# Four interleaved layers on one core: later loads allowed on ScalarE's queue, and a newly searched order

## The chip, the cores and the metric

One core of a Trainium2 chip runs the whole kernel. The metric is the device time of one execution in microseconds (us); smaller is better. The engines are TensorE (PE, with its weight loads PEld), VectorE (DVE), ScalarE (ACT), GpSimd (POOL) and SyncE (SP). SP and ACT begin transfers (DMAs) here.

## What is computed

Four layers in a row on x of 2048 rows and 512 columns: attention, linear attention, attention, linear attention, the second pair with the weights of the first. Both have 32 heads of 16 columns. Cut from the reference:

```python
def _A_ref(x, wqkv, wo):            # H = 32; Dh = 16; W = 256
    q, k, v = qkv[0], qkv[1], qkv[2]
    scores = jnp.einsum("bhqd,bhkd->bhqk", q, k) * (Dh ** -0.5)
    mask = (idx[:, None] - idx[None, :] >= 0) & (idx[:, None] - idx[None, :] < W)
    p = _softmax(jnp.where(mask[None, None], scores, -1e9), axis=-1)
    o = jnp.einsum("bhqk,bhkd->bhqd", p, v)
    return o @ wo                   # heads laid side by side
def _B_ref(x, wqkv, wo):
    phi = lambda t: jnp.where(t > 0, t + 1, jnp.exp(t)) + 1e-6
    pq, pk = phi(q), phi(k)
    kv = jnp.einsum("bhsd,bhse->bhde", pk, v)
    den = jnp.einsum("bhqd,bhd->bhq", pq, pk.sum(s))[..., None] + 1e-6
    return (jnp.einsum("bhqd,bhde->bhqe", pq, kv) / den) @ wo
x = x + _A_ref(_layernorm(x), A_wqkv, A_wo)
x = x + _B_ref(_layernorm(x), B_wqkv, B_wo)
x = x + _A_ref(_layernorm(x), A_wqkv, A_wo)
x = x + _B_ref(_layernorm(x), B_wqkv, B_wo)
```

## The kernel before

The rows are worked in 16 tiles of 128, four tiles to a block. Everything is laid down first as 2583 operations, each with the operations that it needs, the buffers that it holds and the engines that may run it. The string ORDER then says in which order they are emitted, on which engine (P, A, V, G, S for PE, ACT, DVE, POOL, SP; H is a mark for data that has landed) and in which buffer; "F" is a filler, a matmul on the identity whose result nobody reads (line 463). Each engine then runs its instructions strictly in that order, and waits where an instruction's inputs or buffers are not ready. A planner's costs in the code were used when the order was searched; they put nothing into the program.

**Attention.** Lines 806 to 857: q, k and v come from matmuls of 4 x 128 contraction rows (line 537) and are evacuated from PSUM by ACT or DVE (line 527 for q and v, lines 773, 786 and 788 for k, which is spread into two copies with the other head zeroed). 78 rounds per layer each compute scores (line 823, up to 512 columns in each of four banks), take the exponential in two ACT instructions (lines 834 and 837, up to 128x1024 each), and clear what the mask forbids, on POOL (line 857) or DVE (line 852). The weighted sum runs on PE (line 880); DVE normalises (lines 893, 894). Seven buffers pt hold the exponentials. v goes through a staging tile vst into vbd with four DMAs from SP (line 806), and o_sb is transposed into oT by a DMA from SP (line 557).

**Linear attention.** phi takes an exponential on ACT (line 948, 1024), a min/add on DVE or POOL (lines 951, 1027) and a max on DVE (954, 1030). The sums over rows (line 995) close with a chain: kvs (1002), zc and kvn (1042, 1051), the denominator (1078), its reciprocal on ACT (1083, 1084), its spreading (1106) and the product (1110), and last one projection for each tile. Parts of it run beside the next layer's attention.

**Layer norms.** Sums come from DVE (661, or with the residual at 736 to 738), squares from ACT (612, with a read of its accumulator) or DVE (614), the power from POOL (595, 596) or ACT (592, 593), the scaling from POOL (628, 675), DVE (628, 672) or ACT (626).

**Loads.** Four tiles of x and most of A's weights are begun before the order starts, on SP and ACT. The later loads, x tiles 8 to 15 (line 378) and wo of A, the weights and wo of B in halves of 256 KB (line 1133), are operations of their own, and all twelve begin on SP.

Of the kernel before, what the change touches and what calls it, by code (L numbers as in the profile page):

```python
# [214 lines left out]
24S 2G 5G 4G 15H 14H 53V0 0G 11G 58V1 17H 54A 68A1 6G 16H 63V2 3G 59G 55V20 18H 19H 1G 10F0 56P5 60V0 64G 61P1 57A 62V  # L215
9G 69V 2F2 74P0 75A 7V 1F2 70P1 65V0 72P6 71A 66P3 20H 92P7 73A 21H 67V 93P 120P42 94A 80P0 122A 95S 76P6 81V 88P1 121A
77V 89P 23H 22H 78P2 350V0 90A 123G 124P64 82P0 126A 79V 351G 91S 84P1 125A 340V1 133P24 83A 127G 96P6 85V 134A 106P0
10G 97V 104P1 135A 107V 137P26 341G 105V 139A 86P0 138A 146P46 87V 27S 116P1 147A 335V2 98P0 117P 148A 99V 336G 150P42
136V 25S 112P0 345V3 151A 149G 113P 152A 159P64 118A 337V31 140G 102P2 114V 161A 35S 128P1 346G 129P 103V 130P 131P 160A
342V1 163P42 153G 132V 26H 165A 115S 347V2 162G 3F0 188P06 164A 634V1 100P2 189A 166G 141P5 154P4 101V 155P 142P 36H  # L220
143P 190A 635G 144P 28H 352V0 193P02 145V 156P 119S 12G 157P 194A 108P6 158V 167P7 168P 191G 169P 195A 109V 170P 199P04
171V 348P6 200A 353P3 196G 349V 338P7 172S0 354V 343P6 201A 339V 204P02 638V0 379P7 29S 205A 380P 202G 344V 636V32 192G
206A 381V 2F5 210P04 361P6 639G 637S 642V1 362P 211A 208G 110P7 363V 212A 31S 203G 224P02 30H 198G 640V0 225A 383P5 213G
111V 384P 197V 382S 226A 643G 229P06 385V 214P4 215P 230A 646V0 216P 32H 358P5 644V3 231A 647G 217P 228V 235P02 641S
218V 359P 209G 236A 207G 355P7 360V 219P6 645S 237A 933V2 240P04 356P 241A 648V1 220P 239G 357V 221P 649S 232G 222P 233G
242A 246P02 227V 387P7 234G 386S 247A 223V 388P 238G 245V 389V 248A 395P04 13G 664P6 396A 665P 249V 934G 390S 250P7 667V
251P 397A 244G 400P02 666V 252P 243G 401A 941V0 253P 399G 391P6 392P 254V 402A 176S1 405P04 393V 364P7 406A 403G 365P
255P6 407A 366V 394S 410P02 256P 398V 257P 411A 404V 409G 258P 678P7 259V 412A 679P 416P04 680V 260S3 417A 657P3 414G
408V 415G 658P 276V 418A 650P2 264S2 660V 432P06 651P 413V 434A 419G 420V 51S 367P5 421V 368P 433A 659V 422P4 423P 369V
424P 653A 33S 436G 437P06 425P 438A 652V 427P5 428P 426V 429P 439A 430P 442P02 431V 376P4 443A 440G 377P 942G 34H 370P5  # L230
444A 378V 447P06 371P 441V 935V20 448A 682P4 372V 683P 449A 435V 453P02 684V 675P5 454A 676P 446V 451G 685S 452V 450V
455A 2F4 469P60 677V 445V 471A 457V 2F4 474P24 458V 456V 49S 937V1 475A 464P1 459P0 465P 476A 460P 466P 41S 461P 470A
467P 462P 479P24 463V 173P7 472G 480A 39S 468V 174P 481A 175V 484P02 654P6 945V2 936S 655P 485A 482G 373P7 473V 477G
656V 374P 938G 486A 681S 490P04 375V 690P6 483G 491A 691P 946G 487V 492A 177P7 489V 939V0 178P 488G 478V 506P02 692A
494V 495G 493V 507A 693S 943V1 2F4 496P5 179V 501P4 508A 497P 511P06 498P 512A 510V 509G 502P 180V1 499P 47S 503P 513A
500V 504P 181G 516P02 686P5 517A 514V 505V 940S 184V3 518A 3F7 521P06 671P4 45S 48H 687P 522A 519V 947V2 672P 688V 523A
527P20 674V 948S 265P5 266P 529A 524V 526G 661P7 673V 944S 515G 662P 528A 267V 525G 261P6 520V 694P40 663A 689S 531V
532G 262P 695A 530V 533P7 263V 534P 696A 535P 272V0 699P42 538P6 700A 539P 698G 540P 182G01 536P 701A 541P 537V 704P04
273G 705A 542V 952P3 543S1 703G 953P 268V2 706A 709P06 668P2 547S0 954V 669P 710A 274V3 970P3 670V 555S2 711A 715P04
708V 971P 702V 697V 716A 973P7 714G 551S3 972V 974P 707G 712V 717A 731P20 975V 949P6 732A 713V 950P 719G 720V 43S 718V  # L240
733A 951V 2F7 736P42 721P7 722P 738A 723P 734G 726P6 724P 737A 727P 725V 728P 729P 741P24 740G 730V 552P7 739G 743A 553P
977P6 742A 554V 746P40 978P 748A 544P7 979V 545P 747A 744V 752P20 980S 745V 958P6 575V 754A 959P 750G 546V 735G 749V
269G 753A 2F5 768P40 960V 185G 751V 769A 755V 2F7 773P62 756V 757V 8V 774A 186G2 763P5 758P4 764P 567V0 775A 759P 187S
765P 559V1 760P 770A 766P 776G 761P 777G 275S 767V 778P26 270G1 955P0 779A 762V 956P 556P1 780A 957V 976S 783P42 557P
# [104 lines left out]
def build(ctx, tc, A_x, A_wqkv, A_wo, B_x, B_wqkv, B_wo, out, force_safe=False):  # L349
    nc = tc.nc  # L350
# [93 lines left out]
    def fast_network(ctx_f):  # L444
# [681 lines left out]
        def load(b, t, fn):  # L1126
            def f_load(e):
                fn(nc.sync)
            def f_here(e):
                pass  # L1130
            pl.op({"HBM": .3}, f_here, deps=[pl.op({"SP": 1.6}, f_load, after=t)], writes=b)
        def part(w, src, which, k):
            return lambda eng: eng.dma_start(w[:, :, which * D + 256 * k:which * D + 256 * k + 256], wcols(src, which)[:, :, 256 * k:256 * k + 256])
        for i in range(8, NT, 2):
            load(b_x[i:i + 2], 11.0, lambda eng, i=i: load_x(eng, i, 2))
        for k in range(2):
            load([B("woA", k)], 14.0, part(woA, A_wo, 0, k))
# [311 lines left out]
```

## Time and profile before

| | |
|---|---|
| Median of 3 runs (range) | 416.16 us (415.66 to 416.45) |
| Profiled execution, its own time | 416.03 us |
| its span, first to last instruction | 414.3 us |
| PE busy | 395.2 us (95%) |
| ACT busy | 368.8 us (89%) |
| DVE busy | 355.0 us (86%) |
| POOL busy | 239.2 us (58%) |
| Granted TensorE clock, mean | 0.997 |

A busy share is an average over stages that differ. The profile's table by stretches is therefore read first: one stretch from the start to the first exponential of an attention layer, one to the last exponential of that layer, and so on. PE's busy time is modelled and includes the drain of matmuls that overlap, so a PE at 97% is not PE at its peak. Instructions on ACT overlap by about 0.1 us, so that what one adds to the engine's time is the distance from its start to the next start.

### The profile page before, as it was taken

What the parts mean: (1) busy time and instruction counts of PE and PEld (TensorE: products, weight loads), DVE (VectorE), ACT (ScalarE), POOL (GpSimd) and SP (SyncE); (2) the same over time, 40 slices, a digit from 0 to 9 for tenths busy, and PEclk for the clock granted to TensorE, in tenths of its full rate; (3) what the DMA queues carried; (4) which work ended last, traced back from release to release, by engine and by line L of the source; (5) the groups of instructions that cost most, each with busy time, mean ns of one, the idle gap of its engine ahead of it and who ended that gap; (6) DMA issues with size and microseconds to landing.
All of it is one profiled execution on the core that took longest, in us unless ns stands there. A gap on an engine that the chain in (4) does not pass through costs nothing.

```text
span 414.3 us, 15373 instructions
## 1 busy us (share of the span) xinstructions
PE 395.2 (95%) x6277; PEld 219.3 (53%) x6347; DVE 355.0 (86%) x844; ACT 368.8 (89%) x496; POOL 239.2 (58%) x505
## 2 busy tenths in 40 slices
PE   7998999999999999999999999999999999999995
PEld 3565555555555555643565555555555555565342
DVE  5899898888769988689998999998789588889895
ACT  5999999999999999678999999999999999977731
POOL 7578524344576667923774688554427476585432
PEclk9999999999999999999999999999999999999998
DMA  8233226440313122100032212322111311300024
GB/s 245 83 95 100 64 76 110 110 77 24 89 25 80 35 55 26 28 4 0 22 72 41 55 45 64 71 38 53 41 49 34 54 30 40 54 14 14 3 69 138
DMA packets 65306, 24.11 MB, mean 58 GB/s; under 512 B 46160, under 2 KB 65232, under 8 KB 65232
## 3 DMA queue, kind: packets, MB, share of 16 engines
q1 hardware_dynamic: 63168, 21.65, 23.5%
q10 hardware_dynamic: 2064, 1.44, 1.1%
q8 instruction: 50, 0.82, 0.8%
q14 instruction: 24, 0.20, 0.2%
HBM read 6.29 MB, written 2.10 MB: 20 GB/s over the span
## 4 chain that ended last, share of the span: by engine, by line
PE 66%; ACT 15%; DVE 12%; issue 4%; POOL 2%; ACTq 0%; POOLq 0%; DVEq 0%
PE psb L537 41%; PE psb L880 14%; PE psb L823 8%; ACT pt L834 7%; ACT pt L837 7%; DVE pt L852 2%; DVE kall L788 1%; PE psb L995 1%; DVE qT L527 1%; PE psb L566 1%; DVE kall L773 1%; PE psb L463 1%; DVE vst L527 1%; PE psb L1106 1%; DVE ln L661 1%
## 5 line engine op out<-in xcount | busy, mean ns | idle before, releaser
L857 POOL TENSOR_SCALAR_AFFINE_SELECT pt<-pt 128x256 bf16<-128x256 bf16 x285 | 121.3, 453 | 110.2 <-ACT pt L837 66.7
L837 ACT ACTIVATE pt<-psb 128x1024 bf16<-128x1024 f32 (+2 forms) x156 | 156.2, 1017 | 4.4 <-PE psb L823 3.0
L834 ACT ACTIVATE pt<-psb 128x1024 bf16<-128x1024 f32 (+2 forms) x156 | 156.7, 1014 | 3.6 <-PE psb L823 2.3
L880 PEld LDWEIGHTS <-pt 128*128 128x128 bf16 x2880 | 81.4, 96 | 16.5 <-issue 5.0
L880 PE MATMUL psb<-vbd,pt 128*128 128x34 bf16 x2880 | 85.1, 178 | 2.4 <-ACT pt L834 1.0
L537 PE MATMUL psb<-xnT,wA 128*128 128x512 bf16 (+1 forms) x305 | 65.1, 335 | 2.2 <-DVE o_sb L894 0.3
L537 PE MATMUL psb<-wB,xnT 128*128 128x512 bf16 x237 | 62.4, 379 | 1.7 <-issue 0.5
L823 PE MATMUL psb<-qT,kall 32*128 32x256 bf16 (+4 forms) x1664 | 62.6, 242 | 0.6 <-ACT pt L834 0.4
L537 PEld LDWEIGHTS <-xnT 128*128 128x128 bf16 x384 | 33.4, 97 | 37.0 <-issue 5.3
L823 PEld LDWEIGHTS <-kall 32*128 32x128 bf16 x1664 | 28.0, 92 | 45.8 <-issue 42.2
L852 DVE TENSOR_TENSOR pt<-pt,tri 128x512 bf16<-128x512 bf16 (+1 forms) x133 | 49.5, 399 | 2.8 <-ACT pt L837 1.9
L537 PEld LDWEIGHTS <-wA 128*128 128x128 bf16 x320 | 27.4, 97 | 26.1 <-issue 7.7
L537 PE MATMUL psb<-woA,oT 128*128 128x512 bf16 x120 | 32.8, 380 | 1.2 <-issue 0.6
L537 PE MATMUL psb<-wA,xnT 128*128 128x512 bf16 x115 | 32.3, 380 | 1.5 <-ACT pt L837 0.5
L537 PE MATMUL psb<-xnT,wB 128*128 128x512 bf16 x119 | 32.1, 380 | 0.9 <-issue 0.5
L537 PE MATMUL psb<-wkv,pqT 128*128 128x512 bf16 (+1 forms) x126 | 30.2, 373 | 0.5 <-issue 0.2
L894 DVE TENSOR_TENSOR o_sb<-psb,rall 128x256 bf16<-128x256 f32 x64 | 27.2, 424 | 2.4 <-DVE rall L893 0.2
L893 DVE RECIPROCAL rall<-psb 128x16 f32<-128x16 f32 x64 | 16.1, 251 | 13.7 <-PE psb L880 9.4
L661 DVE BATCH_NORM_STATS2 ln<-xres 128x6 f32<-128x512 f32 (+1 forms) x39 | 26.6, 682 | 1.2 <-DMA xres<-in_A_x_dram 1.1
L596 POOL TENSOR_TENSOR ln<-ln,mhalf 128x1 f32<-128x1 f32 x38 | 22.0, 578 | 3.2
L948 ACT ACTIVATE pks<-psb 128x512 bf16<-128x512 f32 x32 | 19.5, 614 | 3.8 <-PE psb L537 3.4
L527 DVE CAST qT<-psb 128x512 bf16<-128x512 f32 (+1 forms) x32 | 19.2, 602 | 3.9 <-PE psb L537 3.7
(133 smaller groups left out, 523.6 us busy)
## 6 DMA issues: line engine op xcount, KB each, us to landing
vbd<-vst SPq DMA_DIRECT2D x128, 34.0 KB, 1.9
wB<-in_B_wqkv_dram SPq DMA_DIRECT2D x6, 256.0 KB, 3.5
out_dram<-ost SPq DMA_DIRECT2D x10, 128.0 KB, 1.8
xres<-in_A_x_dram SPq DMA_DIRECT2D x4, 256.0 KB, 3.2
xnT<-xn SPq DMA_TRANSPOSE x50, 2.4
out_dram<-ost ACTq DMA_DIRECT2D x5, 128.0 KB, 2.8
wA<-in_A_wqkv_dram SPq DMA_DIRECT2D x1, 512.0 KB, 7.5
xres<-in_A_x_dram SPq DMA_DIRECT2D x1, 512.0 KB, 8.7
```

Source lines behind the costliest of these rows:

```text
L527: (nc.scalar.copy if e == "ACT" else nc.vector.tensor_copy)(dst(), src())
L537: nc.tensor.matmul(t["t"][:], lhsT=lhs(c), rhs=rhs(c), start=(c == 0), stop=(c == NCT - 1))
L596: nc.gpsimd.tensor_tensor(out, out, mhalf[:, 0:1], op=ALU.pow)
L661: nc.vector.bn_stats(t["st"], x())
L823: nc.tensor.matmul(psb[:, sT.k + x if x < 2 else sS.k + x - 2, at * 64:(at + w) * 64], lhsT=kbd[half(m)][32 * x:32 * x + 32, tt, m % 4, :, :],
L834: nc.scalar.activation(body[:, 0:2, 0:w_all, :], psb[:, sT.k:sT.k + 2, 0:w_all * 64].rearrange("p x (s c) -> p x s c", c=64), ACT.Exp, sca ...
L837: nc.scalar.activation(body[:, 2:4, 0:w_all, :], psb[:, sS.k:sS.k + 2, 0:w_all * 64].rearrange("p x (s c) -> p x s c", c=64), ACT.Exp, sca ...
L852: nc.vector.tensor_tensor(v, v, mt, op=ALU.mult)
L857: nc.gpsimd.affine_select(out=v, in_=v, compare_op=ALU.is_ge, fill=0.0, base=1 if kind == 0 else -2, pattern=[[0, 4], [2 * sg, 64]], chann ...
L880: nc.tensor.matmul(t["O"][:, x, g, :, :], lhsT=parts[b][0][:, s0:s0 + 2, :], rhs=vbd[half(m)][:, m % 4, :, 4 * tt + g, :], start=(n == 0), ...
L894: nc.vector.tensor_tensor(o_sb[:, u0:u0 + nu, P * tt:P * tt + P].rearrange("p u (h e) -> p u h e", e=DH), Ov[:, :, :, 0:DH], r.to_broadcas ...
L948: nc.scalar.activation(dst(), ps()[:], ACT.Exp)
```

## The change

Each later load may now be begun on SP or ACT (`f_load` takes the queue from the engine in ORDER), the planner's costs and earliest times for these loads are other numbers, and ORDER is another one. The operations are the same 2583.

```diff
         def load(b, t, fn):
             def f_load(e):
-                fn(nc.sync)
+                fn(nc.sync if e == "SP" else nc.scalar)
-            pl.op({"HBM": .3}, f_here, deps=[pl.op({"SP": 1.6}, f_load, after=t)], writes=b)
+            pl.op({"HBM": 1.2}, f_here, deps=[pl.op({"SP": 1.6, "ACT": .62}, f_load, after=t)], writes=b)
...
-            load(b_x[i:i + 2], 11.0, lambda eng, i=i: load_x(eng, i, 2))
+            load(b_x[i:i + 2], 9.2, lambda eng, i=i: load_x(eng, i, 2))
...
-                load([B("wB", which, k)], 18.0, part(wB, B_wqkv, which, k))
+                load([B("wB", which, k)], 9.2, part(wB, B_wqkv, which, k))
...
-            load([B("woB", k)], 50.0, part(woB, B_wo, 0, k))
+            load([B("woB", k)], 15.0, part(woB, B_wo, 0, k))
...
 ORDER = """
-24S 2G 5G 4G 15H 14H 53V0 0G 11G 58V1 17H 54A 68A1 6G 16H 63V2 3G 59G 55V20 18H 19H 1G 10F0 56P5 60V0 64G 61P1 57A 62V
+4G 3G 2G 14H 15H 58V1 9G 53V0 17H 59A 0G 6G 16H 63V2 54A 19H 68A0 55V10 18H 64G 7V 10F0 56P3 60V2 1G 61P5 57V 62V 65V1
...
```

What ORDER does with the loads: one of the twelve stands on ACT, the second half of B's wo, behind 48 exponentials of the first layer; ACT's first load instructions, ahead of the first exponential, are the four that stand there before as well. The other eleven are on SP: one pair of x tiles now stands ahead of the first scattering of v instead of behind the second, and the weights of B and wo of A stand in another order.

What it does with the work: 217 of the 2583 operations change engine (masks above all: 72 from DVE to POOL and 64 from POOL to DVE), 35 fillers stand in place of 45, and most rows within a layer move by a few places. Between the first and the last scores of an attention layer, and outside of them, PE has the same kinds and numbers of operations as before.

ACT in the first attention layer, some 50 exponentials in; kall is the spread k. Before:

```order
67 L837 ACTIVATE pt_147<-psb 128x2x512
68 L834 ACTIVATE pt_147<-psb 128x2x512
69 L786 ACTIVATE kall<-psb,eo 128x256 x2
70 L834 ACTIVATE pt_148<-psb 128x2x512
71 L837 ACTIVATE pt_148<-psb 128x2x512
```

At the same two buffers of the changed kernel:

```order
66 L837 ACTIVATE pt_147<-psb 128x2x512
67 L834 ACTIVATE pt_147<-psb 128x2x512
68 L1133 DMA woB<-in_B_wo_dram 128x4x256
69 L834 ACTIVATE pt_148<-psb 128x2x512
70 L837 ACTIVATE pt_148<-psb 128x2x512
```

The spreading has gone to DVE, and the start of a load stands where it stood.

ACT in the second attention layer, where a layer norm's square (xn, line 612) stood between two pairs of exponentials. Before:

```order
305 L834 ACTIVATE pt_148<-psb 128x2x512
306 L837 ACTIVATE pt_148<-psb 128x2x512
307 L612 ACTIVATE xn,lssq<-xres,lsum 128x512
308 L834 ACTIVATE pt_149<-psb 128x2x512
309 L837 ACTIVATE pt_149<-psb 128x2x512
```

Of the changed kernel:

```order
303 L834 ACTIVATE pt_148<-psb 128x2x512
304 L837 ACTIVATE pt_148<-psb 128x2x512
305 L834 ACTIVATE pt_149<-psb 128x2x512
306 L837 ACTIVATE pt_149<-psb 128x2x512
```

The square has gone to DVE, and the two pairs follow each other.

POOL at about the same place, with layer-norm powers (lines 595, 596), scalings (628) and masks (857). Before:

```order
263 L595 TENSOR_SCALAR lrs<-lssq 128x1
264 L596 TENSOR_TENSOR lrs<-lrs,mhalf 128x1
265 L857 AFFINE_SELECT pt_148<-pt_148 128x4x64
266 L595 TENSOR_SCALAR lrs<-lssq 128x1
267 L596 TENSOR_TENSOR lrs<-lrs,mhalf 128x1
268 L857 AFFINE_SELECT pt_149<-pt_149 128x4x64
269 L628 TENSOR_SCALAR xn<-xres,lnm,lrs 128x512 x2
270 L857 AFFINE_SELECT pt_150<-pt_150 128x4x64
```

Of the changed kernel:

```order
258 L628 TENSOR_SCALAR xn<-xres,lnm,lrs 128x512 x2
259 L857 AFFINE_SELECT pt_148<-pt_148 128x4x64
260 L628 TENSOR_SCALAR xn<-xres,lnm,lrs 128x512
261 L595 TENSOR_SCALAR ln<-ln 128x1
262 L596 TENSOR_TENSOR ln<-ln,mhalf 128x1
263 L857 AFFINE_SELECT pt_149<-pt_149 128x4x64
264 L857 AFFINE_SELECT pt_148<-pt_148 128x4x64 x2
265 L595 TENSOR_SCALAR lrs<-lssq 128x1
266 L596 TENSOR_TENSOR lrs<-lrs,mhalf 128x1
267 L628 TENSOR_SCALAR xn<-xres,lnm,lrs 128x512
268 L857 AFFINE_SELECT pt_150<-pt_150 128x4x64
```

Scalings that were DVE's stand on POOL ahead of masks.

## Rows read from the trace of the kernel before

**Rows 1.** Table by stretches: busy us (instructions) of each engine, granted clock, DMA.

```profile
0.00:11.49 11.49, 8.91 (x52) 3.82 (x53) 6.42 (x29) 6.50 (x17) 7.71 (x28) 1.00 0.74 227
11.49:167.74 156.25, 150.82 (x2686) 87.55 (x2711) 135.20 (x322) 153.08 (x185) 90.64 (x208) 1.00 0.32 69
167.74:206.10 38.36, 37.72 (x415) 19.06 (x419) 32.75 (x84) 30.13 (x65) 20.60 (x30) 1.00 0.06 13
206.10:367.88 161.78, 157.24 (x2710) 89.59 (x2742) 141.37 (x333) 156.33 (x191) 99.87 (x222) 1.00 0.24 49
367.88:414.30 46.42, 40.54 (x420) 19.29 (x424) 39.21 (x78) 22.80 (x44) 20.33 (x21) 0.98 0.15 50
```

**Rows 2.** Waits of ACT from 206.1 to 367.88: total us, times, longest.

```profile
ACT pt L837 <- PE psb L823: 1.8, 5, 0.6
ACT pt L834 <- PE psb L823: 1.6, 4, 0.8
ACT pt L837 <- POOL pt L857: 0.6, 1, 0.6
```

**Rows 3.** Groups of ACT from 11.49 to 167.75: busy us, mean ns, idle before.

```profile
L527 ACT CAST vst<-psb 128x512 bf16<-128x512 f32 x4 | 2.4, 595 | 0.2 <-PE psb L537 0.2
...
L981 ACT CAST vs<-psb 128x512 bf16<-128x512 f32 x3 | 1.8, 597 | 0.2 <-PE psb L537 0.2
...
L527 ACT CAST qT<-psb 128x256 bf16<-128x256 f32 x1 | 0.4, 378 | 0.0
```

**Rows 4.** Timeline of ACT from 51 to 56 us: start, us, instruction.

```profile
51.98 1.02 ACT L834 ACTIVATE pt<-psb 128x1024 bf16<-128x1024 f32 x1
52.89 0.95 ACT L786 ACTIVATE kall<-psb,eo 128x256 bf16<-128x256 f32 x2
53.67 1.04 ACT L834 ACTIVATE pt<-psb 128x1024 bf16<-128x1024 f32 x1
```

**Rows 5.** Timeline of ACT from 396 to 400 us, its queue (ACTq) included.

```profile
396.97 0.59 ACT L1090 CAST pks<-psb 128x512 bf16<-128x512 f32 x1
397.04 0.38 ACTq L731 DMA_DIRECT2D out_dram<-ost  x1
```

**Rows 6.** Timeline of SP's queue from 49 to 53 us.

```profile
49.48 2.53 SPq L557 DMA_TRANSPOSE oT<-o_sb  x2
52.05 0.58 SPq L1133 DMA_DIRECT2D woB<-in_B_wo_dram  x1
```

**Rows 7.** DMA issues on the page: times, KB each, us to landing.

```profile
oT<-o_sb SPq DMA_TRANSPOSE x28, 2.5
```

**Rows 8.** Timeline of ACT from 252 to 255 us.

```profile
252.64 0.74 ACT L612 ACTIVATE xn<-xres,lsum 128x512 bf16<-128x512 f32 x1
253.26 0.22 ACT L612 ACTIVATION_READ_ACCUMULATOR xn<-xres,lsum 128x1 f32 x1
253.47 1.02 ACT L834 ACTIVATE pt<-psb 128x1024 bf16<-128x1024 f32 x1
```

**Rows 9.** Timeline of DVE from 2.9 to 4 us, with the idle time before.

```profile
2.99 0.69 DVE L661 BATCH_NORM_STATS2 ln<-xres 128x6 f32<-128x512 bf16 x1 [1.13 <-DMA xres<-in_A_x_dram]
```

**Rows 10.** Table by stretches of 10 us, and the end of the middle stretch.

```profile
246.00:256.00 10.00, 9.80 (x184) 5.87 (x183) 9.73 (x27) 9.96 (x13) 8.07 (x20) 1.00 0.29 63
256.00:266.00 10.00, 9.84 (x167) 5.38 (x168) 9.87 (x22) 9.86 (x13) 6.32 (x13) 1.00 0.24 55
...
193.00:206.10 13.10, 12.95 (x78) 5.97 (x79) 12.81 (x32) 11.83 (x29) 9.33 (x14) 1.00 0.06 14
```

**Rows 11.** Timelines of PE from 388 to 394 us and of DVE from 399 to 411 us.

```profile
389.32 0.38 PE L463 MATMUL psb<-identb 128*128 128x512 bf16 x1
390.00 0.39 PE L1063 MATMUL psb<-woB,pks 128*128 128x512 bf16 x1 [0.30 <-DVE pks L569]
...
399.55 4.62 DVE L1110 TENSOR_TENSOR pqT<-pqT,psb 128x1024 bf16<-128x1024 bf16 x4
```

**Rows 12.** Groups of POOL from 206.1 to 367.9: busy us, mean ns, idle before.

```profile
L857 POOL TENSOR_SCALAR_AFFINE_SELECT pt<-pt 128x256 bf16<-128x256 bf16 x147 | 62.6, 454 | 49.2 <-ACT pt L837 29.9 <-ACT pt L834 17.0 <-PE psb L537 1.8
L628 POOL TENSOR_SCALAR xn<-xres,lnm,lrs 128x512 bf16<-128x512 f32 x11 | 9.2, 840 | 0.4
L596 POOL TENSOR_TENSOR lrs<-lrs,mhalf 128x1 f32<-128x1 f32 x12 | 7.4, 615 | 1.0
```

**Rows 13.** Line 852 on DVE from 206.1 to 367.88: ns min/median/max, first and last start, forms.

```profile
L852 DVE TENSOR_TENSOR pt<-pt,tri x63: 258/414/653, 215.8 to 367.0; 128x256 bf16<-128x256 bf16 x35, 128x512 bf16<-128x512 bf16 x28
```

More of the change, by code (lines that the diff above doesn't have):

```diff
@@ L220 @@
[L220 to L244, printed above, removed]
@@ new lines @@
+352V0 193P02 145V 156P 31S 341G 157P 194A 167P7 158V 168P 169P 635G 170P 108P6 342V3 195A 199P04 171V 191G 119S 200A
+109V 338P2 353P7 339V 201A 354V 1F3 204P02 32H 638V3 348P7 205A 343P5 176S0 349V 379P6 639G 344V 380P 206A 636V22 198G
+210P04 637S 381V 110P7 211A 209G 642V1 361P6 196G 362P 212A 111V 643G 224P02 363V 382S 225A 192G 383P4 197G 384P 213V
+226A 203V 229P06 208G 644V3 214P5 385V 215P 230A 202G 216P 646V1 217P 645S 358P4 231A 235P02 218V 647G 359P 236A 640V0
+355P7 207G 360V 641S 232G 219P6 237A 648V1 228G 240P04 945V2 356P 234G 649S 241A 12G 220P 357V 221P 222P 242A 239G
@@ new lines @@
+296V 1056P0 1082P26 303A 297V 1051P1 1080G 861S 1084A 1057P 304V 862V3 1052P 1058P 1083A 1053P 305V 863G 1059P 1054P
+314A1 1060V 1088P42 1086G 309P7 1090A 1055V 315G 610P0 1081V 1061S3 581P13 1089A 310V 1093P26 611P 1095A 622P5 623P
+1094A 582P 624V 576P70 326A2 864V1 1096G 1099P24 871A 1062P6 583V 865S 1100A 327G 1063P 316V 628P1 1064V 1101A 629P
+1065S0 577P 612V 630A 589P60 1091G 328V 1113P24 578A 584P11 1098G 1115A 579V 1085G 1102V 590P 1092G 585P 580V 1114A
+1087G 597P01 591V 872G0 598P 586A 1118P24 1116V 613A2 1103P7 873S 592P64 1120A 868V1 593P 599V 1104P 1119A 587V 605P52
@@ new lines @@
+2380P02 2377G 2379V 2124P41 2378G 2382A 2372V 2125P 2160V 2137P70 2368V 2381A 2161V 2132P33 2133P 2373V 2149A 2383V
+2138P 2320V 2134A 2415P24 2150G 2126A 2389P6 2321S 2135V 2390P 2384P0 2136V 2391P 2385P 2139V 2392P 2386P 2393V 2387P
+2416P 2388V 2142P6 2417A 2143P 2414V 2394P00 2418G 2420P11 2127V 2395A 2421P 2151V 2399P31 2422A 2396P0 2400V 2397P
+2144A 2128V 1827P7 2398V 1828P 2401P1 2485V 2419V 2404A0 2402P 2140P4 2145V 2403V 2405G 1837P5 1838P 2409A2 2406V
+2423P02 2146V 2424P 2410G 2141V 2407P1 2425A 2428P20 2408V 2429P 1829A 2411G 2426V 2433P10 2427V 2430A 2434P 1839A
@@ L345 @@
+2508P3 2507S 2521A 2532P1 2540V 2514S 2502A 2533P 2509V 2564P6 2503G3 2562P4 2510A 2565V 2541P2 2528P0 2522G2 2529P
+2534A 2504S 2563V 2543P6 2524P1 2535G0 2525P 2544V 2566P4 2579P5 2536A 2580P 2542V 2570P6 2499A 2571P 2581V1 2567P 2523A
+2545P2 2530V3 2575P3 2572A 2526V2 2531S 2576P 2568V1 2573G3 2546P 2527S 2553P0 2582S 2577V0 2569S 2554P 2574S 2549P1
+2547V2 2555A 2550P 2578A 2548S 2558P2 2556G3 2551V0 2559P 2552A 2560V1 2557S 2561S
 """
@@ L1134, in fast_network @@
         for i in range(8, NT, 2):
-            load(b_x[i:i + 2], 11.0, lambda eng, i=i: load_x(eng, i, 2))
+            load(b_x[i:i + 2], 9.2, lambda eng, i=i: load_x(eng, i, 2))
         for k in range(2):
-            load([B("woA", k)], 14.0, part(woA, A_wo, 0, k))
+            load([B("woA", k)], 10.0, part(woA, A_wo, 0, k))
         for which in (1, 2, 0):
             for k in range(2):
-                load([B("wB", which, k)], 18.0, part(wB, B_wqkv, which, k))
+                load([B("wB", which, k)], 9.2, part(wB, B_wqkv, which, k))
         for k in range(2):
-            load([B("woB", k)], 50.0, part(woB, B_wo, 0, k))
+            load([B("woB", k)], 15.0, part(woB, B_wo, 0, k))
         def prep(key, I):
```

214 lines of the change are left out of this document (110 added, 104 removed).

## The prediction, made before the changed kernel ran

> **What bounds the kernel now.** I read the table by stretches first, because the whole-span shares hide where each engine is the limit. It cuts the span at the first and last exponential of each attention layer [rows 1]. In the two attention stretches, 156.25 and 161.78 us long, ACT is busy 153.08 and 156.33 us: it idles 3.2 and 5.5 us in 318. The reader is to see there that no other engine comes close in a measure that can be trusted. DVE has 135.20 and 141.37 us. PE's 150.82 and 157.24 are modelled ends of overlapping matmuls, and PE spends some of this time on fillers. So in these stretches the time is ACT's work plus the little that ACT waits, and a microsecond of work taken from ACT is worth up to a microsecond. In the 38.36 us between the layers it is otherwise: PE 37.72, DVE 32.75, ACT 30.13. In the last 46.42 us PE and DVE carry a chain, and ACT is half idle.
>
> Next come the waits of ACT in the second attention stretch [rows 2]: 3.4 us on scores from PE in nine waits and 0.6 us on a mask of POOL's in one. So ACT mostly waits for nobody, but when it does, PE came late with scores, and once because POOL held a buffer. This matters for what a freed ACT meets next.
>
> The sum is made against the profiled execution, 416.03 us (span 414.3 and 1.7 around it), 0.13 below the median of 416.16.
>
> **The loads.** The words of the change speak of two loads on ACT ahead of the first exponential. The order shows one load on ACT, half of B's wo, behind 48 exponentials; ahead of the first exponential nothing is added. In the trace the only instruction that waits for a load of x is the very first statistics at 2.99 us, for 1.1 us [rows 9], and that load is unchanged; no later load is ever the last thing waited for. Starting some of them earlier therefore removes no wait: 0 us. What could it cost? On SP nothing that is seen: SP waits for others. On ACT the start of a transfer takes 0.38 to 0.58 us of the queue [rows 5, 6], but [rows 5] also show where it goes: the one at 397.04 is issued 0.07 us after a cast began at 396.97, underneath that cast. At its new place the exponential ahead of it lasts 0.91 us from its start to the next start [rows 4], more than 0.58. The load also waits for the completion of an earlier transfer, one of the two transposes of o_sb that SP began from 49.48 on [rows 6]. They land 2.5 us after their issue [rows 7], so about 52.0 for the first and 53.2 for the second, while ACT comes there at 52.9 at the latest. I take 0; the bounds are 0 and 0.9 (53.2 + 0.58 against 52.89), all of which would stand in front of the exponentials queued behind it.
>
> **ACT's work in the first attention stretch.** By the order, operations that leave ACT there are the k spreading, 0.78 us from its start to the next start [rows 4], one 512-column cast of v (0.60) and two of the linear layer's v (2 x 0.60) [rows 3]: 2.6 us. Those that come are a cast of each of three kinds, 0.60, 0.60 and 0.38 [rows 3]: 1.6. A layer norm's two small instructions leave and two come, and one phi exponential changes places with another across the end. Net -1.0 us.
>
> **In the second.** Two squares of layer norms leave. Each holds ACT from 252.64 to 253.47, 0.83 us with its accumulator read [rows 8]: 1.66. Two 512-column casts leave and one comes (-0.6), a 256-column cast leaves and one comes, and one phi exponential that followed the last exponential now stands ahead of it (+0.6). Net -1.7 us, together -2.7. If the phi is not counted, since it only crosses the cut, -3.3.
>
> **What comes back.** The work goes to DVE and, from DVE, masks and scalings go on to POOL. Around one of the squares, from 246 to 266 us, DVE is busy 9.73 and 9.87 of 10 us beside ACT's 9.96 and 9.86 [rows 10], so there DVE is as full as ACT. What DVE gets must leave it elsewhere for the gain to stay: counting the moved operations with their mean durations, DVE's sum over the second stretch falls by some 2 us and POOL's rises by some 12, as an estimate from the trace's groups. Bounds: nothing comes back, or all 2.7. I take 0.5, nearer to nothing, because the two fullest engines both lose work and the third has 99.87 of 161.78 us [rows 1].
>
> **Head, middle and end.** At the head two statistics change places and the first now waits for a tile that another queue loads; against that ACT and DVE divide the first steps differently. Counting along the chain I find the first exponential between 11.2 and 11.8 against 11.49 [rows 1]: 0, bounds -0.3 and +0.3. Between the layers PE has the same work and is full; DVE gets about 2.4 us more in sum, most of it ahead of 193, where it has room. After that DVE is busy 12.81 of 13.10 us [rows 10], and up to the next scores its sum there grows by 0.1. I take +0.1, bounds -0.5 and +1.0. At the end two fillers go. The one at 389.32 lies in a hole: after it PE still waits 0.30 us for DVE [rows 11], so its removal gives nothing. The four products of 4.62 us that free the last projections [rows 11] stand in the same order. 0, bounds -0.4 and +0.4. The eight other fillers that go lie where ACT and not PE is the limit, or at the start: 0.
>
> **The sum:** 416.03 - 1.0 - 1.7 + 0.5 + 0.1 = 413.9; the single load and the fillers 0.
>
> **Rival: slower, POOL late with the masks.** The place is the second attention stretch from about 247 to 262 us. There POOL's new order puts three scalings that were DVE's ahead of masks, one of them together with a power. A scaling takes 0.84 us and a power 0.62 [rows 12], with its companion some 0.8, so a mask behind them comes about 1.6 us later than it did. PE cannot use those exponentials before, its queue is strict, so the next scores are late, and ACT with them. Against it: POOL waits for ACT through most of its idle time (29.9 and 17.0 us on exponentials [rows 12]), so it usually has masks done early; ACT waited on POOL only once, 0.6 us [rows 2]. For it: exactly this wait exists, and POOL's share in the stretch rises from 62% to some 69%. One such mask costs 1.6, two (3.2) use up the gain of 2.7, so it decides from the second. I price three, 4.8 us: 416.03 - 2.7 + 4.8 + 0.1 = 418.2. Two give 416.6.
>
> **Rival: no change, DVE takes ACT's place.** If DVE, as full as ACT around 246 to 266 us, is what sets the pace wherever it got the work, the 2.7 us return: 416.1 with the 0.1 of the middle. For it, [rows 10]; against it, that over the whole stretch DVE has 20 us of room [rows 1]. The same time follows if POOL's added work lengthens DVE's instructions: a mask on DVE takes from 258 to 653 ns in two shapes [rows 13], so some already run long, by up to 0.24 us beyond the median of 414. Some 13 POOL instructions more in the stretch at 0.24 are 3.1 us, about the gain. The Trainium skill has this as a rule (SBUF — State Buffer, Who interferes with whom): a vector instruction with two SBUF inputs and a GpSimd instruction that reads SBUF share a port pair, and the second to start blocks until the first is through. By it alone the added POOL work would speak for this rival; the trace agrees as far as a median near the minimum of the larger shape and a maximum of 653 allow, that is, long cases exist and are few.
>
> **Rival: more than the sum.** If the search also closed a part of ACT's 8.7 us of waits [rows 1], 2 us of them gives 411.9.
>
> **How the numbers follow.** Forecast 413.9, chance 0.58; more than that, 0.08; no change, 0.15; slower, 0.19. A single measurement of this kernel tells about 0.2% from no change, 0.8 us. The forecast's own spread comes from the returned part (413.4 to 415.3), the load on ACT (up to +0.9) and the middle (-0.5 to +1.0). For 8 in 10 the range takes in the no-change case and two late masks, 416.6, with the load's price, and at the other side the closed waits: 411.9 to 417.2. Faster by over 0.2% 0.66, within 0.2% 0.15, slower 0.19.
>
> **What would show it.** Right: ACT's busy time in the two attention stretches falls by about 1 and 1.7 us and their lengths with it (155.5 and 160.4, if half a microsecond returns), the square stands twice instead of four times among ACT's groups there, the load on ACT starts under an exponential with no gap in the next, the first exponential begins near 11.5, and the middle and the end keep 38.4 and 46.4 us. Wrong: ACT idles more ahead of exponentials, with PE's scores named as the releaser and POOL's masks behind those (POOL), or DVE at 99% over longer parts (DVE); an ACT gap of over half a microsecond around 53 us (the load); or a middle beyond 39.4.

## The result, and the profile after

The changed kernel takes 418.75 us (median of 6 runs, 418.14 to 420.37) where the kernel before took 416.31 in the same runs (415.66 to 416.83): a ratio of 1.0065, with a 95% interval of 1.0044 to 1.0086. It is slower by 2.4 us, and 4.9 us above the forecast of 413.9. Its profiled execution took 418.25 us, with a span of 416.5, against 416.03 and 414.3. Executions of one kernel differ with the mean clock granted to TensorE: of the six, the one at 0.994 took 420.37 us, the others, at 0.998 to 1.000, 418.14 to 419.62; the last section shows what such a fall looks like.

The table by stretches of the changed kernel, cut as [rows 1] are, at the first and the last exponential of each attention layer. The columns are the stretch, its length, the busy us (and instructions) of PE, PEld, DVE, ACT and POOL, the granted clock, the DMA share and GB/s.

```profile
0.00:11.37 11.37, 8.41 (x51) 3.83 (x52) 6.72 (x31) 5.79 (x16) 5.83 (x24) 1.00 0.79 247
11.37:168.98 157.61, 152.72 (x2707) 87.55 (x2706) 134.55 (x318) 152.19 (x183) 96.71 (x216) 1.00 0.30 67
168.98:207.04 38.06, 37.97 (x420) 19.03 (x418) 33.52 (x91) 29.93 (x66) 11.66 (x16) 1.00 0.07 12
207.04:369.44 162.40, 159.29 (x2741) 89.15 (x2741) 140.67 (x331) 155.29 (x188) 110.10 (x242) 1.00 0.24 49
369.44:416.50 47.06, 40.36 (x425) 19.18 (x422) 38.55 (x78) 20.81 (x39) 19.98 (x19) 0.98 0.15 50
```

Set against [rows 1]: the start is 0.12 us shorter, the first attention stretch 1.36 longer, the middle 0.30 shorter, the second attention stretch 0.62 longer, the end 0.64 longer; together the 2.2 us of the span. ACT's busy time fell as it was meant to, 153.08 to 152.19 and 156.33 to 155.29. But ACT idles more: 5.42 us instead of 3.17 in the first stretch and 7.11 instead of 5.45 in the second. Twice as much came back as left. (PE's busy time and its counts can't be compared: records are missing from both traces, more of them before.)

The waits of ACT in the second attention stretch (total us, times, longest), to be held against [rows 2]:

```profile
ACT pt L834 <- PE psb L823: 3.8, 6, 1.0
ACT pt L837 <- PE psb L823: 1.5, 4, 0.6
ACT pt L837 <- DVE o_sb L894: 0.3, 1, 0.3
ACT pt L837 <- DVE okt L919: 0.2, 1, 0.2
```

ACT waits for scores, 5.3 us instead of 3.4. Two places show how that comes about. The first is where a layer norm's square left ACT. ACT from 252 to 257 us (start, us, instruction, in brackets the idle time before and its releaser); the same pairs of exponentials stood around the square of [rows 8]:

```profile
252.51 1.03 ACT L834 ACTIVATE pt<-psb 128x1024 bf16<-128x1024 f32 x1
253.41 1.04 ACT L837 ACTIVATE pt<-psb 128x1024 bf16<-128x1024 f32 x1
255.08 1.02 ACT L834 ACTIVATE pt<-psb 128x1024 bf16<-128x1024 f32 x1 [0.63 <-PE psb L823]
```

The square took 0.83 us there. Now ACT stands idle for 0.63 us at the same place: the next scores come no sooner than they did.

The second place is from 213 to 223 us, where POOL works through layer-norm steps and masks almost without a gap and PE waits for masks. POOL, then PE, then ACT:

```profile
216.53 0.19 POOL L595 TENSOR_SCALAR lrs<-lssq 128x1 f32<-128x1 f32 x1
216.80 0.73 POOL L596 TENSOR_TENSOR lrs<-lrs,mhalf 128x1 f32<-128x1 f32 x1
217.49 1.51 POOL L857 TENSOR_SCALAR_AFFINE_SELECT pt<-pt 128x256 bf16<-128x256 bf16 x4
...
217.13 0.26 PE L880 MATMUL psb<-vbd,pt 128*128 128x34 bf16 x4
217.96 0.19 PE L880 MATMUL psb<-vbd,pt 128*128 128x34 bf16 x1 [0.57 <-POOL pt L857]
218.32 0.64 PE L880 MATMUL psb<-vbd,pt 128*128 128x34 bf16 x19 [0.17 <-POOL pt L857]
...
220.51 0.49 ACT L834 ACTIVATE pt<-psb 128x384 bf16<-128x384 f32 x1 [1.04 <-PE psb L823]
```

The weighted sum on PE (line 880) stands in its strict order, so the scores behind it are late and ACT idles 1.04 us. That is the rival's mechanism, at another place than it named.

And the load that gave the change its name, on ACT's queue among the exponentials:

```profile
51.78 1.15 ACT L834 ACTIVATE pt<-psb 128x1024 bf16<-128x1024 f32 x1
52.29 0.38 ACTq L1133 DMA_DIRECT2D woB<-in_B_wo_dram  x1
53.46 1.02 ACT L834 ACTIVATE pt<-psb 128x1024 bf16<-128x1024 f32 x1 [0.53 <-PE psb L823]
```

It is issued underneath an exponential that runs on until 52.93. The idle time that follows belongs to PE's scores.

### The profile page after: what moved, and what is told of

It is laid out like the page before. It is cut to its first block, busy times and chain, and to the rows that moved or that the text cites. A ratio compares the mean times of both kernels' runs of the same rounds, so it can differ in the third digit from the quotient of the medians.

```text
span 416.5 us, 15442 instructions
## 1 busy us (share of the span) xinstructions
PE 398.7 (96%) x6337; PEld 218.7 (53%) x6337; DVE 354.0 (85%) x847; ACT 364.0 (87%) x486; POOL 244.3 (59%) x515
## 4 chain that ended last, share of the span: by engine, by line
PE 63%; ACT 12%; DVE 11%; issue 4%; POOL 4%; SPq 3%; DMA 2%; ACTq 0%; DVEq 0%; POOLq 0%
PE psb L537 39%; PE psb L880 13%; PE psb L823 7%; ACT pt L837 6%; ACT pt L834 4%; POOL pt L857 2%; SPq L806 2%; DVE pt L852 1%; DVE ln L661 1%; PE psb L995 1%; DVE kall L773 1%; DMA vbd<-vst 1%; DVE xn L672 1%; DVE pqT L1110 1%; PE psb L566 1%
## 5 line engine op out<-in xcount | busy, mean ns | idle before, releaser
L857 POOL TENSOR_SCALAR_AFFINE_SELECT pt<-pt 128x256 bf16<-128x256 bf16 x300 | 123.6, 441 | 89.9 <-ACT pt L837 54.9
L880 PE MATMUL psb<-vbd,pt 128*128 128x34 bf16 x2880 | 86.3, 178 | 3.6 <-ACT pt L834 1.1
L537 PE MATMUL psb<-xnT,wA 128*128 128x512 bf16 (+1 forms) x320 | 67.2, 338 | 1.4 <-ACT pt L834 0.7
L537 PE MATMUL psb<-wB,xnT 128*128 128x512 bf16 x256 | 64.9, 380 | 0.4 <-ACT pt L834 0.3
L852 DVE TENSOR_TENSOR pt<-pt,tri 128x256 bf16<-128x256 bf16 (+1 forms) x125 | 45.6, 392 | 2.5 <-ACT pt L837 1.3
L537 PE MATMUL psb<-wA,xnT 128*128 128x512 bf16 x128 | 34.0, 380 | 0.6 <-ACT pt L837 0.3
L537 PE MATMUL psb<-woA,oT 128*128 128x512 bf16 x128 | 34.0, 381 | 0.4 <-ACT pt L834 0.2
L628 POOL TENSOR_SCALAR xn<-xres,lnm,lrs 128x512 bf16<-128x512 f32 x21 | 16.7, 800 | 12.7 <-ACT lrs L593 12.1
```

Source lines behind the costliest of these rows:

```text
L537: nc.tensor.matmul(t["t"][:], lhsT=lhs(c), rhs=rhs(c), start=(c == 0), stop=(c == NCT - 1))
L628: (nc.vector if e == "DVE" else nc.gpsimd).tensor_scalar(t["xn"][:], xres[:, i, :], lnm[:, c], lrs[:, c], op0=ALU.add, op1=ALU.mult)
L852: nc.vector.tensor_tensor(v, v, mt, op=ALU.mult)
L857: nc.gpsimd.affine_select(out=v, in_=v, compare_op=ALU.is_ge, fill=0.0, base=1 if kind == 0 else -2, pattern=[[0, 4], [2 * sg, 64]], chann ...
L880: nc.tensor.matmul(t["O"][:, x, g, :, :], lhsT=parts[b][0][:, s0:s0 + 2, :], rhs=vbd[half(m)][:, m % 4, :, 4 * tt + g, :], start=(n == 0), ...
```

## The experiments

The theory after the result: in the attention stretches PE, ACT and DVE wait for one another at so many places that work taken from one of them comes back as its wait for the next, while work added to any of them shows. The rivals: ACT's time is worth what the prediction said and something else cost 7 us (late masks on POOL, the load, the engines, the end); or one other engine is the bound alone. The times are medians with their ratio to the kernel before, run on the same chip between them.

**Order and engines apart.** ORDER holds both. In the first run the changed order keeps the old engines, in the second the old order gets the new ones. Only letters change, 217 of them (and in the second run `f_load`, so that the load can begin on ACT); three of those of the first run:

```diff
-653V 1564V 1345G
+653A 1564A 1345V
```

> The changed kernel's order of operations, with all 217 operations that changed engine back on the engine they had before (the load of wo of B on SP too). If the engine changes (masks and scalings put on POOL) cost the 2.4 us, this comes out near 416.3, and the waits of ACT for scores from 207 to 223 us, which grew by some 1.5 us, shrink again. If the order in which PE, POOL and ACT take their work is the cause, it stays at 418 to 419.5: ACT gets 2 us of work back and PE's order still puts more between two scores.

> The order of before, with the 217 operations on the engines of the changed kernel. If the engines are the cause, 418 to 419.5. If the order is the cause and the relief of ACT is worth what the prediction said, 413.5 to 415. If the relief of ACT is given back as waits for PE's scores and nothing else is wrong, 416 to 416.8.

Measured: 430.22 us (1.0333, 1.0309 to 1.0356) and 430.91 us (1.0352, 1.0326 to 1.0378). Both mixtures are 14 us slower than before and, by the ratios, 11 to 12 slower than the changed kernel. So neither half is the cause by itself, and none of the theories had expected it: either order is far better with its own engines, and its effect is not a sum of its moves. That is a first blow to any prediction which adds up moves.

**The load.** One letter of the changed kernel:

```diff
-51A
+51S
```

> The changed kernel with the one load that ScalarE begins put back on SP, at the same place of the order. Prediction's term for it was 0 with a bound of 0.9 us. The trace shows it issued underneath an exponential, 0.38 us long, with the next exponential waiting for scores and not for it, so 0: 418.75 within 0.4. If the load costs what its bound allows, 417.9.

Measured: 418.75 us (1.0052, 1.0037 to 1.0067), the same as with the load on ACT. The load costs nothing, as the prediction had it. ACT's gap of 0.53 us behind it, near the place where the prediction would have blamed the load, is 0.53 us without it too.

**Late masks.** Two ways to have the masks of 215 to 221 us earlier: four of them (and at 144 us one mask and two steps ahead of it) on DVE; or, in the second run, the two pairs that are late placed on POOL ahead of the layer-norm steps, with no engine changed:

```diff
-1332G 1336G 1358G 1345G 1044G 573G 333G
+1332V 1336V 1358V 1345V 1044V 573V 333V
...
+1332G 1336G
 1561G
...
-1332G
...
-1336G
```

> The changed kernel with seven POOL operations on DVE: the four masks of exponentials that PE waits for between 215 and 221 us (two of them were on POOL before as well), the mask that it waits for at 144 us, and a scaling and a min/add of phi that stand ahead of that mask on POOL (1 and 2 us there). If late masks on POOL are the cause, the waits of ACT of 1.04 and 0.87 us near 220.5 and 222.3 and of 0.51 near 145.3 fall to 0.2 each and the time to some 417 (418.75 less 1.7). If PE is late there for its own order, the time stays within 0.4 of 418.75. If DVE is the fuller engine and loses as much, it rises to 419 or more.

> The changed kernel with two pairs of masks of POOL ahead of the layer-norm steps that stand before them (their exponentials end at 208.8 and 210.4, POOL cleared them from 215.2 and 217.5 on, and PE waited for the second until 218.3). No work changes engine. If late masks cost what the waits near 220.5 and 222.3 show, 417 to 417.8. If the wait only passes on to the scalings that now come later, or to PE's next product, 418.4 or more.

Measured: 418.90 us (1.0059, 1.0037 to 1.0081) and 419.49 us (1.0081, 1.0051 to 1.0111). Neither is faster than the changed kernel. In the first, ACT's gaps of 1.04 and 0.87 us came down to one of 0.48, yet the stretch is 162.19 us instead of 162.40, and the first one, where a wait of 0.51 fell to 0.22 and one of 0.36 stands three microseconds later instead, is 0.5 longer. In the second, the gap of 1.04 is gone and the next two grew from 0.87 and 0.33 to 1.20 and 0.91. There the layer norm's scalings, now behind the masks, are late, and with them the transposing DMA that a product waits for:

```profile
222.20 0.60 PE L537 MATMUL psb<-xnT,wA 128*128 128x256 bf16 x4
223.21 1.02 PE L537 MATMUL psb<-xnT,wA 128*128 128x512 bf16 x3 [0.41 <-DMA xnT<-xn]
```

So the late masks are real, and making these earlier is worth nothing by itself: where they no longer hold PE, something else does.

**ACT's relief alone.** The order and engines of before, but for the 15 operations of the attention layers that left ACT or came to it:

```diff
-118A 653A 583A 599A 1070A 1316A 1564A 2182A 1598A 1921A   871G 607V 630V 1292V 1327V
+118V 653V 583V 599V 1070G 1316V 1564V 2182V 1598V 1921V   871A 607A 630A 1292A 1327A
```

> The order of before and its engines, but for the 15 operations of the two attention layers that the changed kernel moves off ACT or onto it (casts, one spreading, two squares, two small layer-norm steps): ACT is relieved, net 2.7 us by the prediction, nothing else changes. If the prediction's step holds that a microsecond of work taken from ACT is worth up to a microsecond, 414 to 415. If PE is just as full and its scores come no sooner, 416.3 to 417, with ACT's waits for scores longer by what its work is shorter. If DVE, which gets the work, sets the pace, 417.5 or more.

Measured: 419.90 us (1.0078, 1.0058 to 1.0099), 3.7 us slower than before. ACT's busy time falls by 0.3 and 1.6 us in the two stretches, which get 1.9 and 2.1 us longer. One square shows how. ACT, DVE and PE of this run, where [rows 8] had the square on ACT; DVE's line 614 is the square, now twice in a row:

```profile
254.11 1.05 ACT L837 ACTIVATE pt<-psb 128x1024 bf16<-128x1024 f32 x1
255.85 1.02 ACT L834 ACTIVATE pt<-psb 128x1024 bf16<-128x1024 f32 x1 [0.69 <-PE psb L823]
...
255.20 1.21 DVE L773 TENSOR_TENSOR kall<-psb,eo 128x1024 bf16<-128x1024 f32 x1
256.33 0.74 DVE L614 SCALAR_TENSOR_TENSOR xn<-xres,lnm 128x512 bf16<-128x512 f32 x1
...
256.99 0.75 DVE L614 SCALAR_TENSOR_TENSOR xn<-xres,lnm 128x512 bf16<-128x512 f32 x1
...
259.03 0.42 DVE L894 TENSOR_TENSOR o_sb<-psb,rall 128x256 bf16<-128x256 f32 x1
...
257.84 1.02 PE L537 MATMUL psb<-wA,xnT 128*128 128x512 bf16 x4
259.51 0.40 PE L823 MATMUL psb<-qT,kall 32*128 32x64 bf16 x12 [0.65 <-DVE o_sb L894]
```

The square's 0.83 us off ACT return at once as 0.69 us of waiting for scores. On DVE it stands ahead of the normalising of o_sb (lines 893, 894), whose bank the next scores need: they wait 0.65 us. At this place what was taken from ACT gains nothing, and most of what was put on DVE comes back as a wait.

**The same moves undone in the changed kernel**, the reverse of that diff:

> The changed kernel with the 15 operations of the attention layers that moved off ACT or onto it back on the engine of before; masks, fillers, stores and order as changed. In the order of before these moves cost 3.7 us. If they cost the same here, so that the rest of the change gains, 415 to 416. If ACT's added 2 us show in full, as work added to ACT did, 420.5 to 421.5. If each order fits its own engines only, the same side, 420 or more, with ACT waiting less than now and working more.

Measured: 421.73 us (1.0106, 1.0073 to 1.0139), by the ratios 1.7 us slower than the changed kernel, though the two intervals just overlap. ACT works 1.25 and 1.44 us more in the two stretches. It idles 6.9 us instead of 5.4 in the first, where this trace also has a fall of the clock from 24.19 us on, and 6.7 instead of 7.1 in the second. In the order of before these moves cost; in the changed order it is their undoing that costs, if anything. Each order fits its own engines.

**Work added.** Ten places, five in each attention layer of the kernel before, on one engine at a time: pairs of fillers on PE (one of ten in the diff), pairs of exponentials on ACT or of products on DVE into a scratch tile, single masks on POOL (the diff has ACT's places).

```diff
-376P4
+2F4 376P4
...
+        if o.n in (194, 443, 705, 821, 1078, 1398, 1650, 1746, 2024, 2329):
+            self.extra()
```

> The kernel before with 10 pairs of fillers more on PE, five pairs in each attention layer, each ahead of a product and in its bank: 20 x 0.216 = 4.3 us of PE time. If PE's time in these stretches is mostly slack (ACT the only bound), 417 or less, by under 1 us. If PE is as much the bound as ACT, more than 2 of the 4.3 us show.

> The kernel before with 10 pairs of 128x256 exponentials into a scratch tile more on ACT, spread as the fillers of the PE run: some 10 x 0.5 = 5 us of ACT time by the distance of starts, which its trace will tell. If ACT alone is the bound, nearly all of it shows: 420.5 to 421.5. If PE and ACT share the bound, about half.

> The kernel before with 10 pairs of 128x256 bf16 products into a scratch tile more on DVE, some 10 x 0.5 = 5 us of DVE time, spread in the same way. By the room that DVE has over the two stretches (20 us in each) it should cost under 1 us; if DVE is the third bound where it is full, 1 to 3 us.

> The kernel before with 10 masks more on POOL, on a scratch tile, each ahead of a mask, 10 x 0.42 = 4.2 us. POOL is 58% busy. If late masks are what counts (the rival of the prediction), 1.5 us or more; if PE uses most masks late enough, under 0.8: 417 or less.

The 0.216 us is the usual distance from one filler's start to the next one's.

| added to | busy time added | time | ratio to before |
|---|---|---|---|
| PE | 20 x 0.216 = 4.3 us | 419.42 us, +3.2 | 1.0073 (1.0050 to 1.0096) |
| ACT | 368.8 to 375.1 = 6.3 us | 422.14 us, +5.9 | 1.0131 (1.0110 to 1.0152) |
| DVE | 355.0 to 359.8 = 4.8 us | 419.51 us, +3.3 | 1.0075 (1.0055 to 1.0096) |
| POOL | 10 x 0.445 = 4.5 us | 415.92 us, -0.9 | 0.9987 (0.9973 to 1.0000) |

Work added costs three quarters of itself on PE, nine tenths on ACT and two thirds on DVE, though DVE is idle for 20 us in each stretch; on POOL it costs nothing. DVE's 3.3 us are more than either expectation allowed. So at these places three engines have little slack and the fourth has room.

**Work left out, and given to nobody.** In the diff first ACT's exponentials (lines 834 and 837), then PE's products (line 537), then DVE's masks; the lists are cut short.

```diff
+                w_all = w_all // 2 if pl.cur in (397, 443, 705, 821) else w_all
...
+                    if pl.cur in (376, 377, 668, 669) and c in (1, 2):
+                        continue
...
-        o.fn(e)
+        if o.n not in (197, 441, 708, 819):
+            o.fn(e)
```

> The kernel before with less work on ACT and none of it given to another engine: 10 exponentials, five in each attention layer, take only the left half of their columns (the other half of the buffer keeps older exponentials, so the weighted sums of these rounds are other numbers). That is some 10 x 0.43 = 4.3 us off ACT. If a microsecond off ACT is worth nearly a microsecond when no other engine has to take it, 412 to 413. If PE's scores come no sooner, so that ACT waits instead, 415 to 416.3.

> The kernel before with less work on PE: ten products in the two attention layers leave out two of their four contraction steps (so these products are other numbers): 10 x 0.43 = 4.3 us off PE. If PE is a bound by itself, 412 to 413.5; if PE and ACT bound each other, 414.5 to 416.3.

> Both together: the ten half exponentials and the ten products with two steps left out, at about the same places. If PE and ACT bound each other, the gain is clearly more than the sum of the two single ones: 412 to 413, 3 to 4 us. If only one of them is the bound, the gain is that one's alone; if DVE is a third bound, it is under 2 us.

> The kernel before with less work on DVE: ten masks of DVE, five in each attention layer, are left out (so forbidden places of these rounds keep their exponentials), about 4.0 us by their durations in the trace of before. Taking some 4 us off ACT, off PE, or off both, moved the time by under 1 us. If DVE is the engine that holds the rest, 413 to 415. If the order as a whole holds it, 416 to 416.8.

> All three together: the ten half exponentials, the ten products with two steps left out, the ten masks left out. If the three engines bind one another and nothing else does, 412.5 to 413.5, near the 4 us that each of them is relieved of. If something else holds the pace (transfers, buffers, the order between the places), 415 or more.

| taken from | busy time taken | time | ratio to before | first, second stretch |
|---|---|---|---|---|
| ACT | 368.8 to 365.3 = 3.5 us | 416.09 us | 0.9983 (0.9968 to 0.9998) | 155.97, 162.01 us |
| PE | 20 x 0.216 = 4.3 us | 416.60 us | 1.0006 (0.9991 to 1.0021) | 155.77, 162.12 us |
| ACT and PE | both | 415.88 us | 0.9980 (0.9964 to 0.9996) | 155.10, 163.16 us |
| DVE | 355.0 to 352.2 = 2.8 us | 417.08 us | 1.0008 (0.9998 to 1.0018) | 157.69, 161.65 us |
| all three | all | 414.57 us | 0.9948 (0.9929 to 0.9968) | 156.15, 161.75 us |

Before, the stretches are 156.25 and 161.78 us. One engine relieved of 3 to 4 us gives at most 0.7; with less on DVE the time was, if anything, longer. Only where all three are relieved does something come out that is beyond doubt, 2.1 us, which is less than any one of them lost (its profiled execution, 416.19 us, was the slowest of its six, so the stretches don't show it). That is the opposite of the table above: a microsecond added to one of these engines costs 0.7 to 0.9, and one taken from it gives 0 to 0.2. PE's 416.60 and DVE's 417.08 us lie just above what was named for no gain. Two other expectations failed in kind. ACT and PE together don't give clearly more than the two singly, so they are not a pair that bound each other alone. And all three together, at 414.57 us, lie between the two cases that were named: the three engines bind one another, and something else holds the pace as well. In the first stretch ACT and PE together give 1.15 us and singly 0.28 and 0.48, but 0.30 of the 1.15 is a first exponential that came that much later, so there too the sum of the two is all that shows.

Two disturbances stand in these numbers. Around 115 us, with the next mask of DVE left out, a product of PE waited 1.24 us for an exponential, which it had not done before; such a wait is part of both runs with less on DVE. And in the second stretch a product waited for a transposing DMA for 1.3 to 1.6 us in four runs with some work left out (PE less, ACT and PE less, all three, no fillers), and not in the kernel before, nor where ACT alone or DVE alone did less, nor where work was added. In the run without fillers:

```profile
222.37 0.60 PE L537 MATMUL psb<-xnT,wA 128*128 128x256 bf16 x4
224.45 1.02 PE L537 MATMUL psb<-xnT,wA 128*128 128x512 bf16 x3 [1.48 <-DMA xnT<-xn]
```

So at least at that place a fourth party keeps the pace, SP's transposing DMA. POOL's scaling ahead of it isn't late: it ends at 217.18 with PE less and at 217.66 before. The transposing DMA behind it begins at 219.24 with PE less, against 218.03; with ACT and PE less it begins earlier, at 217.49, but takes 4.02 us to land instead of 2.93. Why was not settled, and each of these is a single execution. With ACT and PE less the wait of 1.55 us is followed by a fall of the granted clock to 0.50 from 222.09 to 225.50 us, which is part of the 163.16 us of that stretch.

**Fillers and stores.** All 45 fillers of the kernel before left out (the plan's tokens with F); and the changed kernel with the eleven result stores that changed queue put back:

```diff
-10F0
...
-2F2
...
-1F2
...
-2569S 2574S 2578A 2499A 2504S 2510A 2514S 2523A 2536A 2548S 2552A
+2569A 2574A 2578S 2499S 2504A 2510S 2514A 2523S 2536S 2548A 2552S
```

> The kernel before without any of its 45 fillers (13 at the start, 26 in the first attention layer, 4 in the second, 2 at the end). The prediction put the ten that go at 0. If they lie in holes of PE, 416 to 417 and the stretches keep their lengths within 0.3 us; if they take PE's time where it is full, the first attention stretch is shorter by 1 us or more; if PE's clock falls for want of them, the granted clock of the first 30 us is under 1.0 and the time is longer.

> The changed kernel with the eleven stores of the result that changed queue (SP to ACT and ACT to SP) back on the queue of before, all else as it is. The last stretch is 0.64 us longer than before, and 0.8 us more of it lie behind DVE's last instruction, where the stores stand close on SP. If the queues are the cause, 418.0 to 418.3; if DVE's last steps come late and the stores with them, 418.75 within 0.3.

Measured without fillers: 420.63 us (1.0094, 1.0067 to 1.0122). In the profiled execution the start takes 13.27 us instead of 11.49, the first attention stretch 156.50 instead of 156.25 and the end 46.36 instead of 46.42; the second attention stretch, 162.74 instead of 161.78, holds the wait of 1.48 us shown above. So where 26 fillers, 26 x 0.216 = 5.6 us of PE, are gone from the first attention stretch nothing is gained: they lie in holes. At the start they matter, which the last section shows. The traced execution, 419.05 us, is the fastest of the four and has a mean clock of 0.999; the other three, 420.39 to 421.17, have 0.990 and 0.991. No execution of the kernel before is under 0.997. So the fillers may be worth something in the clock as well, but where it fell in those three no trace shows.

Measured with the stores back: 420.34 us (1.0092, 1.0068 to 1.0111), not faster than the changed kernel, and outside both expectations. All four executions have a mean clock of 0.993, and the changed kernel's own at 0.994 took 420.37 as well; the trace has a fall of the clock ahead of the last stores, from 395.86 us on. Behind DVE's last instruction 5.0 us are left, as against 4.8 in the changed kernel and 4.0 before. So the stores' queues aren't what lengthens the end.

## Why the prediction was wrong

**The loads: right.** The one load on ACT runs beneath an exponential, and on SP the time is the same. (There are fourteen later loads, not twelve: four of x, two of wo of A, six and two of B's weights. Thirteen stay on SP.)

**ACT's work: right in kind, smaller in busy time.** The squares stand twice instead of four times in the second stretch, and POOL is busy 110.10 us there, 68% against the 69% that was reckoned. ACT's busy time fell by 0.89 and 1.04 us, against 1.0 and 1.7.

**What that is worth: the step that failed.** The prediction read from [rows 1] that "a microsecond of work taken from ACT is worth up to a microsecond" and let 0.5 of 2.7 us come back. It took the 3.2 and 5.5 us that ACT idles as the only room, and DVE's 20 us as room for what ACT gives away. The runs show in its place: 3.5 us taken from ACT and given to nobody are worth 0.7; the 15 moves made in the order of before cost 3.7; work added to DVE costs two thirds of itself. ACT's idle time of 2% said that ACT was nearly always needed. It did not say that ACT alone was needed, and [rows 10], where DVE and ACT are at 97 to 100% side by side, with PE's modelled 98%, already spoke against it; the prediction used them for one rival only. For the two stretches together it forecast -2.2 us; +1.98 came, which is 4.2 of the 4.3 us by which the profiled execution missed. The spread that it gave for the returned part was too narrow even by its own bound: with all 2.7 back the sum is 416.1, not 415.3. The Trainium skill (Perfetto Trace Analysis, Identifying the Most-Contended Engine) takes the engine of highest occupancy as the one to work on first, with other measures for TensorE. Here that engine is ACT, and 3.5 us off it gave 0.7: by the runs with work added PE and DVE are bounds as well, so the rule alone does not pay here.

**The rivals.** The slower one had the right sign and mechanism: late masks of POOL exist and PE waits for them, 0.57 us at 217.96. Its place was wrong (218 to 222 us and 144, not 247 to 262), and so was its price: with these masks early again the time is no shorter. The one of no change, DVE in ACT's place, comes nearest in substance, since DVE does bind. It was sized as if DVE would only take back the gain; the relief alone, in the order of before, turned a reckoned gain of 2.7 us into a loss of 3.7. That POOL's added work would lengthen DVE's instructions did not show: with ten more masks on POOL DVE was busy 355.2 us instead of 355.0, and the time was no longer.

**Head and middle: right.** 11.37 and 38.06 us, within the bounds of -0.3 to 0.3 and -0.5 to 1.0. The fillers that go were put at 0, and the traced execution without any supports that for those of the first attention layer.

**The end: 0.64 where 0 with bounds of 0.4 was said.** The four products of 4.62 us in [rows 11] take as long as they did. The step was the order alone: it looked at the products and not at what follows them. After DVE's last instruction, which ends at 410.26 before and at 411.69 after, 4.0 us of the span are left before and 4.8 after. Which of the late stores makes it was not settled; that their queue does was refuted. The two fillers that go at the end were put at 0 as well, since one lies in a hole. Behind the place of that filler PE now idles for 0.27, 0.43 and 0.33 us between 391.9 and 395.1, and in two later runs of this order the clock fell right behind these holes. Whether the fillers would have prevented that was not tested.

**What stays open.** How the 2.4 us divide among single moves can't be told, since moves don't add: undoing the eleven stores, the fifteen moves of ACT or all 217 changes of engine, or putting seven of POOL's steps on DVE (five of them stood there before), leaves the changed kernel as slow or makes it slower by up to 11 us. ORDER names buffers too, and their part was not separated from that of the order. The traces show where the time goes (1.36, 0.62 and 0.64 us in three stretches) and as what (ACT's waits for PE's scores); that this order is a worse fit by 0.65%, and that none of the single waits that were tested is the culprit, is what the runs support. That the three engines bind one another was shown in the kernel before; that this is what makes the changed one slower is argued from it.

## What to carry to other kernels

Before a microsecond off the fullest engine is counted as gain, ask what a microsecond added to each of the others costs: a few scratch instructions in a handful of places measure it in one run per engine. Where, as here, three engines each answer with two thirds or more, expect relief of one to be worth little and work handed from one to another to cost; slack shown by such a run (POOL's here), and not idle time, is room. In this kernel, whose order was searched as a whole, a sum over moved instructions predicted neither size nor sign.

## What the runs showed of the hardware

The fillers at the start do bring PE to its full clock sooner. PE from 10 to 13 us in the run without fillers, where it had done only transposes and products of 256 columns since 6.17 us:

```profile
10.39 0.63 PE L566 MATMUL psb<-identb,xn 128*128 128x128 bf16 x4
10.82 1.91 PE L537 MATMUL psb<-wA,xnT 128*128 128x512 bf16 x4
```

In the kernel before, with 13 fillers there, the same rows read:

```profile
9.71 0.40 PE L566 MATMUL psb<-identb,xn 128*128 128x128 bf16 x4
9.94 1.03 PE L537 MATMUL psb<-wA,xnT 128*128 128x512 bf16 x4
```

Four products take 1.91 us instead of 1.03, near the ratio of TensorE's two levels of 1.2 and 2.4 GHz, and the first exponential comes 1.8 us later. The granted clock reads 1.00 for this stretch in both traces, but the record of the clock begins only at 13.29 us without fillers (at 5.97 before), and ahead of its first entry the column has nothing to go by. The durations tell it.

The clock can also fall within the run. Of the twenty kept traces four show it ahead of the last microseconds, those with a mean clock of 0.992 or 0.993; the other sixteen, at 0.997 and above, don't. The same eight products in the changed kernel, then in the one with the stores back, and last the table of the latter over the fall (the granted clock is the 0.50, the lower of the two levels):

```profile
395.05 1.89 PE L537 MATMUL psb<-wkv,pqT 128*128 128x512 bf16 x8 [0.33 <-DVE pqT L1110]
...
395.54 3.30 PE L537 MATMUL psb<-wkv,pqT 128*128 128x512 bf16 x8 [0.33 <-DVE pqT L1110]
...
395.86:399.27 3.41, 3.41 (x16) 0.87 (x13) 3.29 (x4) 0.00 (x0) 0.00 (x0) 0.50 0.00 0
```

From the end of the second attention layer to DVE's last instruction the run takes 43.88 us instead of 42.25. Ahead of the falls PE had waited: for 0.27, 0.43 and 0.33 us here, for 1.55 us with ACT and PE less, for 0.70 us with the moves of ACT undone. The changed kernel's trace has the three short waits too and no fall, so they alone don't bring it about. The changed kernel has one execution of six at 0.994, so the clock doesn't explain the 2.4 us.
